# Attention into two mixtures of experts: which queue starts the small layout transfers, and which the stores of finished rows

## The chip, the cores and the metric

The kernel runs on one core of one Trainium2 chip. Times are microseconds (us) that the device took for the whole program. Five engines work side by side, each through its own instructions in order: TensorE (PE, with its weight loads as PEld), VectorE (DVE), ScalarE (ACT), GpSimd (POOL) and SyncE (SP). DMA transfers are started by an instruction on SP, ACT or POOL and then run on the core's 16 DMA engines; "to landing" is the time from that instruction to the arrival of the last byte. "Granted clock" is the share of its full speed that TensorE was given in a stretch.

## The reference, cut to what matters

A linear recurrence with complex decay runs over 768 tokens for 4 batches of 8 heads of 48 channels. Its output, as 3072 rows of 384, goes through a mixture of 8 experts and then a second one with a skip rule:

```python
for t in range(S):
    ar, ai = (a_re_n[:, :, t, :, None], a_im_n[:, :, t, :, None])
    new_re = ar * S_re - ai * S_im
    new_im = ar * S_im + ai * S_re
    kv = np.einsum('bhd,bhe->bhde', k[:, :, t], v[:, :, t])
    S_re, S_im = (new_re + kv, new_im)
    y[:, :, t] = np.einsum('bhd,bhde->bhe', q[:, :, t], S_re)
x = np.ascontiguousarray(y.transpose(0, 2, 1, 3)).reshape(B * S, H * D)
x = _moe_ref(x=x, **moe_kwargs)       # argmax expert, relu(x @ w1[e]) @ w2[e], times gate
return _moe2_ref(x=x, **moe2_kwargs)  # rows with x @ w_skip > 0 alone: x + the same
```

## The kernel before

**Stages.** `prefix` forms the running products P of the decays, up to about 165 us of the span. `attention` follows, up to about 389 us, where its last store starts. Then come the first and the second mixture of experts. The change lies in `attention`.

**Attention.** The tokens are cut into 12 units of 256 (the loop's n, three per batch), each of two chunks of 128 (24 steps i). For each unit `prod(n)` makes, on DVE and ACT, Qo = q·P and Ko = k/P, with channels on the partitions in an order in which three blocks of 128 hold eight heads. For the scores, TensorE needs the same numbers with 96 partitions (real and imaginary part of one head below each other) and the head as an index: the second layout, `qst` and `kst`. `relayout` makes it by transfers within the on-chip memory, five for each of the two parts: two of 48 partitions x 3 heads (144 KB), one of 32 partitions (64 KB) and two of 16 partitions (16 KB each). They are numbered 0 to 9; numbers 3, 4, 8 and 9 are the 16 KB ones. `qst` has three buffers, `kst` two.

**One step i** of the loop (line 692): state update on PE (`kv`), turning of Ko (`ktr`), the rows of the chunk before (`rows`, tile yp), the decay of the state on DVE (tiles Vt, T, St; it needs the chunk-end products `pb`), the scores of the next chunk (`scores`, tile sc, line 562, which needs all of that unit's `kst` and `qst`), their masks on DVE (sm), the store of the chunk before (`store`: xtp, xo, and a transfer to memory), and the turning of the state (`turn_state`: Stp, Ssb). Between these pieces the loop draws pieces of `prod(n + 2)`, called `fill`: unit n + 2 is made while unit n runs, Ko at the end of it.

**Queues.** SP starts all relayout transfers but five of unit 0 (`QP`, line 56). POOL starts the loads of k, q, v and pb and the stores of rows 0 to 19 (line 659); SP starts the last four stores. In the built program a transfer of SP or ACT takes the next of eight semaphores, one of POOL the next of another eight, and each waits until the earlier transfer on its semaphore has landed. Instructions of one queue start in order, so what waits for DVE or PE holds up what stands behind it.

Of the kernel before, what the change touches and what calls it, by code (L numbers as in the profile page):

```python
# [52 lines left out]
H0,H1=(6, 2)  # L53
HV=2
WU=4
QP,KP=({0: (5, 6, 7, 8, 9), 2: ()}, {2: ()})
FAST=((0, 2, 0, 7), (2, 3, 2, 4), (2, 4, 2, 2), (7, 4, 0, 0))
R_LATE, R_H1, R_H2, I_T, R_T, R_H3, H6, H9, H11, EF, EP = (3, 0.3, 1.5, 5, 2.5, 1.2, 5, 9, 11, 20, 3)
TAIL=2
# [4 lines left out]
XS=20  # L64
# [362 lines left out]
def attention(nc, tc, k, early, split):  # L427

    P = k.P
    with ExitStack() as c0:  # L430
# [208 lines left out]
        def store(i):  # L639

            x = X[i]
            for pair in range(4):
                nc.tensor.matmul(
                    lgb[32 * pair:32 * pair + E, 0:128], k.wgp[:, pair], x.xt[:, pair], start=True, stop=True,
                    tile_position=(0, 32 * pair))
            x.lt = wk.tile([128, 128], F32, name="lt", tag="lt", bufs=1)
            nc.scalar.activation(out=x.lt, in_=lgb[:, 0:128], func=AF.Copy)
            ps = psA.tile([128, 4, 2, 64], F32, name="xtp", tag="xt")
            for pair in range(4):
                nc.tensor.transpose(  # L650
                    ps[:, pair].rearrange("p r d -> p (r d)")[:, 0:112], x.xt[:, pair], k.idn[:112, :112])
            if i == XALT:
                xo = ip.tile([128, C, UG], F32, name="xo", tag="k").rearrange("p t g -> p (t g)")[:, 0:384]
            else:
                pool, tag = (wk, "xo") if i < ni - 1 else (up, "D0")
                xo = pool.tile([128, 384], F32, name="xo", tag=tag, bufs=1)
            nc.scalar.activation(  # L657
                out=xo.rearrange("p (a r d) -> p a r d", a=4, r=2), in_=ps[:, :, :, 0:48], func=AF.Copy)
            (nc.sync if i >= XS else nc.gpsimd).dma_start(out=k.x0[i * 128:i * 128 + 128], in_=xo)  # L659

        def logits(i):
            nc.tensor.matmul(lgb[:, 128:136], X[i].lt, k.sum4, start=True, stop=True)
# [29 lines left out]
        for i in range(ni):  # L692
# [37 lines left out]
            if i > 0:  # L730
                store(i - 1)
# [9 lines left out]
        emit(islice(split, SA[3]))  # L741
        logits(ni - 2)
        store(ni - 1)
        emit(islice(split, SA[4]))
        logits(ni - 1)
# [1193 lines left out]
```

## Time and profile before

| | us |
|---|---|
| median of 3 timed runs | 750.12 |
| the three runs | 747.13, 750.12, 752.61 |
| the profiled execution | 753.02 |
| its span, first to last instruction | 751.3 |
| PE busy | 638.0 (85%) |
| DVE busy | 600.3 (80%) |
| ACT busy | 425.3 (57%) |
| POOL busy | 203.7 (27%) |
| mean granted TensorE clock | 0.926 |

All rows below are from one profiled execution; times in them count from the start of its span. Busy time on an engine says how long it worked, not whether anyone waited for it; who waited is read from the chain of waits and from the idle time in square brackets behind an instruction, with what ended it. SP and POOL are listed with the instructions that start transfers.

### The profile page before, as it was taken

How to read it: one execution, taken by the hardware profiler on the slowest of the kernel's cores; microseconds unless marked ns; L12 is line 12 of the kernel's file. 1: busy time of each engine (PE TensorE's matmuls, PEld its weight loads, DVE VectorE, ACT ScalarE, POOL GpSimd, SP SyncE). 2: the span in 40 equal slices, each digit the busy share in tenths (PEclk: the TensorE clock that was granted, in tenths of full speed). 3: DMA queues.
4: the chain of work that ended last, by engine and by line, in shares of the span. 5: the costliest groups of instructions: out<-in, count | busy, mean ns of one | idle time of the engine just before them, and what ended most of it. 6: DMA issues, size and time to landing. Idle time of an engine off the chain costs nothing.

```text
span 751.3 us, 13960 instructions
## 1 busy us (share of the span) xinstructions
PE 638.0 (85%) x5007; PEld 550.5 (73%) x5007; DVE 600.3 (80%) x1391; ACT 425.3 (57%) x847; POOL 203.7 (27%) x296
## 2 busy tenths in 40 slices
PE   1787886515999979999978999999999999899991
PEld 0444444313888868887868899999999997678991
DVE  5989999995898967999878876566776668789980
ACT  7757786623356543554363365566655566488860
POOL 6200000004023221221534254334474443520110
PEclk9989998855699996999988999999999999999996
DMA  5769945008579886886634021263111148488900
GB/s 213 273 193 295 296 137 168 1 0 208 147 201 239 227 218 139 231 214 175 201 133 178 23 64 43 71 233 150 43 43 43 43 168 330 162 295 318 324 37 12
DMA packets 46045, 121.94 MB, mean 162 GB/s; under 512 B 12104, under 2 KB 30962, under 8 KB 41616
## 3 DMA queue, kind: packets, MB, share of 16 engines
q1 hardware_dynamic: 31200, 71.52, 31.3%
q0 software_dynamic: 14768, 49.45, 20.4%
q8 instruction: 41, 0.67, 0.4%
q14 instruction: 36, 0.29, 0.1%
HBM read 116.84 MB, written 16.52 MB: 178 GB/s over the span
## 4 chain that ended last, share of the span: by engine, by line
PE 53%; DVE 14%; DMA 11%; issue 9%; ACT 8%; POOL 2%; SPq 1%; POOLq 0%; DVEq 0%; ACTq 0%
PE yps L1402 13%; PE hps L1355 11%; PE sc L562 6%; DMA out_dram<-z,idx 5%; DVE t L381 3%; PE m L278 3%; PE yp L632 2%; PE yp L634 2%; DMA kst<-Ko 2%; PE wps L592 2%; DVE P L386 2%; PE wps L591 2%; PE xtp L650 1%; PE u L278 1%; PE ktp L546 1%
## 5 line engine op out<-in xcount | busy, mean ns | idle before, releaser
L149 DVE TENSOR_TENSOR wlo<-wraw,whi 128x768 fp32r<-128x768 f32 (+1 forms) x95 | 82.5, 903 | 13.8 <-ACT whi L148 12.8
L149 DVE TENSOR_TENSOR w<-P,w 128x768 fp32r<-128x768 f32 (+1 forms) x95 | 82.5, 903 | 11.0 <-ACT w L148 10.1
L278 PE MATMUL m<-sq,idn 128*128 128x288 f32 x112 | 40.0, 486 | 42.2 <-ACT sq L271 42.2
L148 ACT ACTIVATE whi<-wraw 128x768 fp32r<-128x768 f32 (+1 forms) x95 | 71.0, 802 | 0.0
L148 ACT ACTIVATE w<-P 128x768 fp32r<-128x768 f32 (+1 forms) x95 | 70.7, 800 | 0.0
L1362 DVE SCALAR_TENSOR_TENSOR hl<-hps,hh 128x512 fp32r<-128x512 f32 x48 | 33.1, 690 | 46.0 <-ACT hh L1361 45.9
L562 PE MATMUL sc<-qst,kst 96*128 96x128 f32 x384 | 56.4, 303 | 12.0 <-DMA kst<-Ko 9.7
L562 PEld LDWEIGHTS sc<-qst,kst 96*128 96x128 f32 x384 | 50.5, 210 | 18.1 <-issue 8.1
L1361 ACT ACTIVATE hh<-hps 128x512 fp32r<-128x512 f32 x48 | 28.7, 598 | 61.9 <-PE hps L1355 61.9
L278 PEld LDWEIGHTS m<-sq,idn 128*128 128x128 f32 x112 | 22.2, 216 | 55.1 <-ACT sq L271 29.6
L381 DVE TENSOR_TENSOR t<-P,n 128x288 f32<-128x288 f32 x127 | 57.7, 454 | 4.4 <-ACT n L332 1.9
L1390 POOL DMA_INDIRECT out_dram<-y,idx x26 | 28.0, 1076 | 111.5 <-ACT y L1389 95.4
L553 ACT ACTIVATE kt<-ktp 128x384 f32<-128x384 f32 x40 | 19.5, 488 | 59.5 <-PE ktp L552 59.4
L1402 PE MATMUL yps<-w,hh 128*128 128x394 f32 x192 | 51.4, 349 | 0.0
L1355 PE MATMUL hps<-xh,w 128*128 128x256 f32 x288 | 46.3, 295 | 4.0 <-DVE hl L1362 2.8
L1355 PEld LDWEIGHTS hps<-xh,w 128*128 128x128 f32 x288 | 41.0, 200 | 4.7 <-DVE hl L1362 3.0
L568 DVE TENSOR_TENSOR sm<-sc,tri 128x512 f32<-128x512 f32 x48 | 32.6, 680 | 12.6 <-PE sc L562 12.2
L467 POOL DMA_DIRECT2D qst<-Qo x5 | 2.8, 559 | 146.2 <-DVE D L503 146.2
L659 POOL DMA_DIRECT2D x<-xo x20 | 11.3, 565 | 108.3 <-ACT xo L657 108.3
L386 DVE TENSOR_TENSOR P<-t 128x144 f32<-128x144 f32 x127 | 37.9, 299 | 0.1
L496 DVE TENSOR_TENSOR Qo<-q,P 128x516 f32<-128x516 f32 (+5 forms) x52 | 36.7, 784 | 0.0
L632 PE MATMUL yp<-sm,v 128*64 128x128 f32 (+1 forms) x384 | 36.5, 279 | 0.0
(372 smaller groups left out, 1888.4 us busy)
## 6 DMA issues: line engine op xcount, KB each, us to landing
P<-in_w2t_dram SPq DMA_DIRECT2D x8, 1536.0 KB, 6.7
P<-in_v_dram SPq DMA_DIRECT2D x8, 1536.0 KB, 7.9
wraw<-in_v_dram SPq DMA_DIRECT2D x8, 1536.0 KB, 8.4
raw<-in_a_dram SPq DMA_DIRECT2D x15, 576.0 KB, 5.8
kst<-Ko SPq DMA_DIRECT2D x48, 144.0 KB, 3.7
qst<-Qo SPq DMA_DIRECT2D x46, 144.0 KB, 5.5
k<-in_k_dram POOLq DMA_DIRECT2D x12, 384.0 KB, 6.3
q<-in_q_dram POOLq DMA_DIRECT2D x12, 384.0 KB, 7.6
```

What stands on the lines that cost most here:

```text
L148: self.nc.scalar.activation(out=hi, in_=r, func=AF.Copy)
L149: self.nc.vector.tensor_tensor(lo, r, hi.bitcast(F32), op=ALU.subtract)
L278: nc.tensor.matmul(x, k.idn, sq[:, h, :, r], start=r == 0, stop=last and r == 1)
L381: nc.vector.tensor_tensor(t1, P.at(t - 1)[:, ::-1].unsqueeze(2).to_broadcast([128, 2, 2, G]), pairs, op=ALU.mult)
L386: nc.vector.tensor_tensor(P.at(t), t1[:, 0], t1[:, 1], op=ALU.add)
L496: nc.vector.tensor_tensor(V(Qo[:, r])[:, s], P4(d.q[:, s]), P4(p[:, :, r]), op=ALU.mult)
L562: nc.tensor.matmul(ps[:, h], U[n].kst[:, 4 * g + h, cs], U[n].qst[:, 4 * g + h, cs], start=True, stop=True)
L568: nc.vector.tensor_tensor(X[i].sm[:, 4 * g:4 * g + 4], X[i].sc[g], k.mask.to_broadcast([128, 4, 128]), op=ALU.mult)
L632: nc.tensor.matmul(o, U[n].v[:, c, h * 48:h * 48 + M], x.sm[:, h], start=zero, stop=True)
L1355: nc.tensor.matmul(ps[:, i], self.W.w1(s, wp_, j)[:, f * 128:f * 128 + 128], x[xp_][:, j], start=n == 0, stop=n == 8)
L1362: nc.vector.scalar_tensor_tensor(out=hl, in0=ps, scalar=0.0, in1=hh.bitcast(F32), op0=ALU.max, op1=ALU.subtract)
L1402: nc.tensor.matmul(ps, hs[kk // 2][hp][:, kk % 2, us], self.W.w2(s, wp_, kk, Weights.DW), start=n == 0, stop=n == 23)
```

## The change

The four 16 KB transfers of each relayout go from SP's queue to POOL's, for Q of units 1 to 11 and for K of all 12 units: 92 transfers. Unit 0's Q keeps its five on POOL. The 20 stores of rows that POOL started are now started by ACT. Nothing is computed otherwise.

```diff
-QP,KP=({0: (5, 6, 7, 8, 9), 2: ()}, {2: ()})
+SMALL = (3, 4, 8, 9)
+QP,KP=({0: (5, 6, 7, 8, 9), 2: SMALL}, {2: SMALL})
...
-            (nc.sync if i >= XS else nc.gpsimd).dma_start(out=k.x0[i * 128:i * 128 + 128], in_=xo)
+            (nc.sync if i >= XS else nc.scalar).dma_start(out=k.x0[i * 128:i * 128 + 128], in_=xo)
```

Line numbers behind line 56 grow by one. Three places show how the instructions now stand.

POOL at the start of attention, before (pd are the chunk-end products on their way to memory, pb their copies coming back; the first k and q are unit 2's, the second unit 3's):

```order
L467 DMA qst<-Qo 48x3x256 x2
L467 DMA qst<-Qo 32x512
L467 DMA qst<-Qo 16x256 x2
L406 DMA pd<-e_sb 48x1x384
L454 DMA pb<-pd 64x2x384
L454 DMA pb<-pd 48x2x384
L454 DMA pb<-pd 64x2x384
L454 DMA pb<-pd 48x2x384
L443 DMA k<-in_k_dram 128x768
L443 DMA q<-in_q_dram 128x768
L443 DMA k<-in_k_dram 128x768
L443 DMA q<-in_q_dram 128x768
```

And now, from pd on:

```order
L407 DMA pd<-e_sb 48x1x384
L468 DMA qst<-Qo 16x256 x4
L468 DMA kst<-Ko 16x256 x4
L455 DMA pb<-pd 64x2x384
L455 DMA pb<-pd 48x2x384
L455 DMA pb<-pd 64x2x384
L455 DMA pb<-pd 48x2x384
L444 DMA k<-in_k_dram 128x768
L444 DMA q<-in_q_dram 128x768
L468 DMA qst<-Qo 16x256 x4
L444 DMA k<-in_k_dram 128x768
L444 DMA q<-in_q_dram 128x768
```

Four transfers of kst of unit 0 now stand ahead of pd; pb and the k and q of unit 2 stand behind qst and kst of unit 1, and unit 3's k and q behind qst of unit 2.

POOL in one unit of the loop, before:

```order
L659 DMA x_61<-xo 128x384
L448 DMA v<-in_v_dram 128x768
L454 DMA pb<-pd 64x2x384
L454 DMA pb<-pd 48x2x384
L659 DMA x_61<-xo 128x384
L443 DMA k<-in_k_dram 128x768
L443 DMA q<-in_q_dram 128x768
```

And now:

```order
L468 DMA kst<-Ko 16x256 x4
L449 DMA v<-in_v_dram 128x768
L455 DMA pb<-pd 64x2x384
L455 DMA pb<-pd 48x2x384
L468 DMA qst<-Qo 16x256 x4
L444 DMA k<-in_k_dram 128x768
L444 DMA q<-in_q_dram 128x768
```

The two stores are gone; the loads of k and q wait behind qst (that is, for Qo) where they waited behind a store.

ACT at the end of a step, now (xo is the copy of the finished rows, Ssb that of the turned state, D the first step of a unit's `prod`):

```order
L648 ACTIVATE lt<-lgb 128x128
L658 ACTIVATE xo<-xtp 128x384
L660 DMA x_61<-xo 128x384
L618 ACTIVATE Ssb<-Stp 96x448
L489 ACTIVATE D_2205<-P_153 128x516
```

The store is the one new row; on PE and DVE no instruction moves. SP keeps six transfers of each relayout where it had ten.

## Rows read from the trace of the kernel before

**Rows 1.** Stretches: PE, PEld, DVE, ACT, POOL busy (count), clock, DMA share, GB/s.

```profile
200.00:217.80 17.80, 17.80 (x241) 15.57 (x240) 16.60 (x29) 9.21 (x21) 3.95 (x7) 1.00 0.69 174
...
262.70:278.60 15.90, 13.74 (x176) 11.97 (x176) 13.08 (x22) 8.47 (x19) 3.94 (x7) 1.00 0.83 209
278.60:295.70 17.10, 14.39 (x95) 12.27 (x96) 8.95 (x14) 4.56 (x11) 1.35 (x3) 0.50 0.60 145
```

**Rows 2.** Chain that ended last, 220 to 300: start, us, what.

```profile
225.34 1.98 PE sc L562 x16
...
231.35 1.98 PE sc L562 x16
...
238.47 1.98 PE sc L562 x16
...
274.69 7.34 DMA kst<-Ko
```

**Rows 3.** PE in order of time, scores alone: start, us, what, [idle before <-releaser].

```profile
270.47 2.05 PE L562 MATMUL sc<-qst,kst 96*128 96x128 f32 x16
...
279.31 0.77 PE L562 MATMUL sc<-qst,kst 96*128 96x128 f32 x2 [2.77 <-DMA kst<-Ko]
282.08 3.35 PE L562 MATMUL sc<-qst,kst 96*128 96x128 f32 x14 [2.01 <-DMA kst<-Ko]
...
294.51 2.60 PE L562 MATMUL sc<-qst,kst 96*128 96x128 f32 x16
```

**Rows 4.** SP in order of time, the relayouts of unit 6.

```profile
260.19 9.76 SPq L467 DMA_DIRECT2D qst<-Qo  x10
270.06 7.68 SPq L467 DMA_DIRECT2D kst<-Ko  x10
```

**Rows 5.** DVE in order of time, the second part of unit 6's Ko.

```profile
265.56 1.53 DVE L509 TENSOR_TENSOR Ko<-D,P 128x516 f32<-128x516 f32 x2
```

**Rows 6.** POOL in order of time, the loads between 270 and 276.

```profile
271.38 1.20 POOL L454 DMA_DIRECT2D pb<-pd  x2
...
274.79 0.55 POOL L443 DMA_DIRECT2D k<-in_k_dram  x1
```

**Rows 7.** Line 467 (relayout): duration in ns min/median/max, starts; landing.

```profile
L467 SPq DMA_DIRECT2D kst<-Ko x120: 507/620/1554, 173.4 to 360.6; - x120
...
L467 POOL DMA_DIRECT2D qst<-Qo x5: 496/519/657, 169.1 to 171.3; - x5
...
DMA to landing us min/median/max: 1.8/4.5/8.6
```

**Rows 8.** Waits of PE, 180 to 380: us in total, times, longest.

```profile
PE sc L562 <- DMA kst<-Ko: 9.7, 5, 4.3
```

**Rows 9.** POOL at the start of attention: q of unit 2.

```profile
178.66 0.55 POOL L443 DMA_DIRECT2D q<-in_q_dram  x1
```

**Rows 10.** DVE at the start of attention.

```profile
181.81 2.80 DVE L509 TENSOR_TENSOR Ko<-D,P 128x516 f32<-128x516 f32 x4
...
192.25 1.51 DVE L496 TENSOR_TENSOR Qo<-q,P 128x516 f32<-128x516 f32 x2
...
199.37 0.56 DVE L602 TENSOR_TENSOR Vt<-wps,pb 112x384 f32<-112x384 f32 x1 [1.32 <-PE wps L592]
...
201.44 0.35 DVE L607 TENSOR_TENSOR St<-T,Vt 112x192 f32<-112x192 f32 x1
```

**Rows 11.** PE at the start of attention.

```profile
181.98 0.77 PE L562 MATMUL sc<-qst,kst 96*128 96x128 f32 x2 [4.31 <-DMA kst<-Ko]
...
204.61 0.55 PE L615 MATMUL Stp<-idn,St 112*96 112x112 f32 x4
```

**Rows 12.** DMA issues: KB each, median us to landing.

```profile
q<-in_q_dram POOLq DMA_DIRECT2D x12, 384.0 KB, 7.6
```

**Rows 13.** Line 659 (stores), those that SP started.

```profile
L659 SPq DMA_DIRECT2D x<-xo x4: 332/342/352, 371.5 to 388.6; - x4
```

**Rows 14.** Waits of ACT, 180 to 380: us in total, times, longest.

```profile
ACT kt L553 <- PE ktp L552: 56.5, 27, 9.2
```

## The prediction, made before the changed kernel ran

> **What bounds the kernel now.** The change touches attention alone, so I read its stretches first, then the chain of waits through them, then the engines named there in order of time. Between 200.0 and 217.8 PE is busy for all of the 17.80 us at full clock, and DVE for 16.60 of them [rows 1]: PE sets the pace, DVE is close behind. In the chain, the scores of three successive steps start at 225.34, 231.35 and 238.47 [rows 2]; these are the steps at the end of a batch, which have less to do, and they take 6.01 and 7.12 us. The step that answers to them one batch later reads otherwise: scores at 270.47, the next ones at 279.31, and of these the last fourteen records only at 282.08, after idle times of 2.77 and 2.01 us that `kst` ended [rows 3]. The chain has there 7.34 us of a transfer into `kst` that SP started at 274.69 [rows 2]. From 278.6 to 295.7 the granted clock is 0.50, that is the lower of the two levels, 1.2 GHz [rows 1], after PE had stood. So one late `kst`, unit 6's, costs twice.
>
> Why was it late? DVE had the second part of Ko ready at 265.56 + 1.53 = 267.09 [rows 5]. SP was still busy with Q of the same unit, ten transfers from 260.19 on, and began with K at 270.06, ten more over 7.68 us [rows 4]. By then POOL started pb at 271.38 and k at 274.79 [rows 6], and K's last transfers ran beside those loads. SP's starts are the queue that unit 6 waited for.
>
> **The change, part by part.**
>
> *SP: 92 starts fewer.* A start takes 0.62 us at the median [rows 7], a relayout of ten 6.2 us, one of six 3.7. For unit 6: Q's six are through before K's data are there at 267.1; K's second part then needs three starts, the last at 267.1 + 2 x 0.62 = 268.3, or 272.8 landed at the median of 4.5, and 276.9 at the longest of 8.6 [rows 7]. The scores need it at 270.47 + 6.01 = 276.5 [rows 2, 3]. It is in time at the median by 3.7 us, and 0.4 late at the worst. What this is worth:
> - The wait: the step's scores ended at 282.08 + 3.35 = 285.43; without it at 276.5 + 2.05 = 278.5 [rows 3]. That is 6.9 us.
> - The clock: from the end of these scores to the next ones passed 294.51 - 285.43 = 9.1 us [rows 3]; one batch earlier, at full clock, 238.47 - (231.35 + 1.98) = 5.1 [rows 2]. That is 4.0 us more, if PE doesn't stand there any longer.
> - Other waits for `kst` inside the loop: of 9.7 us in all [rows 8], 4.8 are unit 6's [rows 3] and 4.3 are unit 0's [rows 11]; 0.6 is left.
>
> Together 11.5 us less. The bounds: from 2.5 us (four starts of 0.62 saved, and K still in the crowd of loads) to 11.5.
>
> *POOL: 92 starts more, 20 fewer.* At 0.52 us [rows 7] that is 48 us more over 200 us on an engine that was busy 3.95 of 17.8 [rows 1]: nothing in the loop, where the small transfers of K come before the unit's v and pb. k and q of unit n + 3 now wait for Qo of unit n + 2 instead of a store; both came in the same microseconds, and they are needed a unit later. Cost 0.
>
> *POOL at the start.* Here order matters. q of unit 2 was started at 178.66 [rows 9]. Now it stands behind unit 1's K, which DVE finishes at 181.81 + 2.80 = 184.61 [rows 10]: two small starts (1.0), four of pb (2.4, at 0.60 each [rows 6]) and k (0.55) later q starts at 188.6, ten microseconds later than before, and lands at the median of 7.6 us [rows 12] at 196.2. DVE wanted it at 192.25 [rows 10]: 4.0 us late, with everything behind it on DVE. Of these DVE makes up the 1.32 us that it stood before Vt at 199.37, so St, done at 201.44 + 0.35 = 201.8, comes at 204.5 [rows 10]. PE turns that state at 204.61 [rows 11]. So it is just hidden, and DVE works off the rest at about 1.2 us in two steps (17.80 - 16.60 [rows 1]). In exchange the first scores lose most of their 4.31 us wait [rows 11], because pb, k and q no longer run beside unit 0's K; that lead ends at the same St. I take 0 for the start. Bounds: 3 us gained, if St doesn't hold PE; 8 us lost, if the 4.0 pass on to PE in full and the standing costs another stretch of low clock at unit 6's price of 4.0.
>
> *ACT: 20 starts more.* SP's stores took 0.34 us each [rows 13], so 6.8 us in all, in front of Ssb and of the next unit's squares. ACT waits 2.1 us on average (56.5 / 27) before each kt that it waits for [rows 14]; the start fits in there. Cost 0; with the longest relayout start, 1.55 us [rows 7], it would still fit. The store's semaphore was last used a relayout earlier, and the next xo is a step away, so no new wait is on its path.
>
> **The sum.** 753.0 - 11.5 = 741.5 us against the profiled execution, which lies 2.9 above the median of the runs shown and 0.4 above the highest. Against the median it gives 738.6. I predict **740**.
>
> **Rivals.**
> *The 16 DMA engines set the landing, not SP.* From 262.7 to 278.6 their share is 0.83 [rows 1], the last K transfer needed 7.34 us [rows 2] against a median of 4.5, and the bytes stay. Then only the starts are saved: 2.5 us at unit 6, the low clock stays, time 750. Against it: K would start and mostly land before pb and k do [rows 5, 6]. The Trainium skill says this in DMA: Bandwidth & Descriptors, section "Issuing engines are not separate DMA queues": transfers of all issuing engines share the 16 engines, and issuing from several saves only the issue time, usually small beside the transfer. Here the trace agrees only in part: ten starts at 0.62 us are longer than the median landing of 4.5. By the page alone the result would be "no change". Chance 0.16.
> *The start costs.* POOL's new order makes DVE 4 us late and PE feels it: 741.5 + 4 to 8 = 745.5 to 749.5. For it: DVE has only 1.2 us in 17.8 to spare. Against: the state is turned late enough. Chance 0.14.
> *ACT becomes the bound: slower.* In-order ACT holds kt, xt and Ssb behind a store's start. If that took longer than the 2.1 us of slack, each microsecond more would cost 20; 1% slower than the median (757.6) is reached at a hold of 2.1 + (757.6 - 741.5) / 20 = 2.9 us, and at 3.5 us it is 769.5. For it: no ACT start is in the trace at all. Against it: SP's take 0.34, and no start of a relayout of K over 1.55 [rows 7, 13]. Chance 0.08.
> *K's wait moves to another unit*, with a new place and the same 11 us: 753. Chance 0.04.
> The forecast keeps 0.58.
>
> **How the numbers follow.** 1% of 750.1 is 7.5 us, about what a measurement of this kernel can tell from no change: faster means below 742.6, slower above 757.6. The forecast, with its offset to the median, is 736 to 743 and nearly all faster; both middle rivals and the moved wait are within 1%, the ACT rival is slower, to which I add 0.02 for what I haven't seen. Faster 0.57, same 0.33, slower 0.10. The range goes down to 734 (the start's 3 us gained, and a little more), and up to 752, which takes in the first two rivals and leaves out the slow one.
>
> **What will show it.** SP's relayouts take about 4 us each, with gaps between them; unit 6's K starts within 1 us of Ko; the scores of the step after 270 stand under 1 us; no stretch at 0.50 begins between 270 and 300; the wait of PE for `kst` falls from 9.7 to under 3 us. At the start, DVE's first Qo of unit 2 is released by q of unit 2, some 3 to 5 us later than before, and the state turned at 204.61 moves by under 1 us. ACT's store start is under 0.7 us. I am wrong if unit 6's K starts early and yet lands after its scores want it, if the late q moves PE by several microseconds, or if a low clock shows up in another place.

## The result, and the profile after

The changed kernel takes **743.65 us** (median of 12 runs, 742.09 to 747.09) against 751.58 for the kernel before in the same job (12 runs, 745.38 to 755.61): ratio 0.9909 [0.988, 0.9939]. That is 7.9 us less at the medians, where 11.5 were summed. The ratios, with their 95% intervals, are estimated apart from the medians and leave out executions over 1.5% above the fastest of their kernel, so they are not quite the quotients of the medians. The profiled execution took 745.46 us; its span is 743.7 us, against 751.3 before, and its mean granted clock 0.932 against 0.926.

At unit 6 the profile shows what was forecast, though the queue held K back in a way that the prediction did not name. The stretches of [rows 1], the same columns, in the changed kernel:

```profile
200.00:217.80 17.80, 17.80 (x240) 15.57 (x241) 17.34 (x29) 9.45 (x22) 8.14 (x16) 1.00 0.85 218
262.70:278.60 15.90, 15.90 (x204) 13.99 (x203) 14.71 (x25) 8.39 (x20) 6.83 (x13) 1.00 0.87 232
278.60:295.70 17.10, 16.89 (x221) 14.57 (x219) 16.08 (x27) 9.53 (x23) 7.17 (x14) 1.00 0.96 238
```

PE no longer stands in the second stretch, and the third has the clock at 1.00 (2.4 GHz) instead of 0.50. Note the first: DVE is now busy for 17.34 of 17.80 us, where it was 16.60.

SP in order of time at unit 6, which answers to [rows 4]:

```profile
256.94 4.29 SPq L468 DMA_DIRECT2D qst<-Qo  x6
265.05 4.29 SPq L468 DMA_DIRECT2D kst<-Ko  x6
```

Q's six starts end 3.8 us before K's begin; K no longer queues behind Q, and its second three starts wait only for DVE, which has that part of Ko at 265.42 + 1.54 = 266.96 (267.09 in [rows 5]). The scores on PE, which answer to [rows 3]:

```profile
269.74 2.05 PE L563 MATMUL sc<-qst,kst 96*128 96x128 f32 x16
...
275.74 2.05 PE L563 MATMUL sc<-qst,kst 96*128 96x128 f32 x16
...
282.86 2.05 PE L563 MATMUL sc<-qst,kst 96*128 96x128 f32 x16
```

The step after 269.74 comes 6.00 us later and in one piece. Its end is 277.79 instead of 285.43, and the next scores start at 282.86 instead of 294.51: **11.65 us gained** by there. PE's waits from 180 to 380 (us, times, longest), beside [rows 8]:

```profile
PE Stp L616 <- DVE St L608: 5.1, 1, 5.1
...
PE lgb L905 <- DVE aoh L899: 1.2, 1, 1.2
...
PE sc L563 <- DMA kst<-Ko: 0.2, 1, 0.2
```

The wait for `kst` has gone from 9.7 to 0.2 us. Two larger ones are new in attention: 5.1 us for St at the start, and 1.2 us for `aoh`, a tile of the routing.

**What had held SP.** SP's own waits in the kernel before, 180 to 380 (us, times, longest):

```profile
SPq L467 <- DMA qst<-Qo: 8.6, 8, 2.7
...
SPq L467 <- DMA kst<-Ko: 6.7, 9, 2.0
```

The longest of them lies at unit 6. By the trace's semaphore records, the ninth of Q's ten starts, at 268.77, waited on semaphore 101, which Q's first, started at 260.19, signals when it has landed; that was at 268.75. SP stood for 2.67 us before that start. K began 2.97 us after the second part of its data was there (270.06 - 267.09), so the greater part of that was this wait and not time spent on starting: with ten starts and eight semaphores, the ninth takes the first one's. In the changed kernel, with six starts, SP's waits in the same stretch have one for a relayout transfer, of 0.3 us.

**Where gain was given back: the routing.** After step 16 of the scores PE needs `aoh` for the first batch's routing. PE in the kernel before:

```profile
318.84 2.05 PE L562 MATMUL sc<-qst,kst 96*128 96x128 f32 x16
...
321.58 0.33 PE L904 MATMUL lgb<-aoh,onesb 128*128 128x96 bf16 x1
...
327.66 0.60 PE L562 MATMUL sc<-qst,kst 96*128 96x128 f32 x3
```

and in the changed kernel:

```profile
307.29 2.05 PE L563 MATMUL sc<-qst,kst 96*128 96x128 f32 x16
...
311.07 0.33 PE L905 MATMUL lgb<-aoh,onesb 128*128 128x96 bf16 x1 [1.19 <-DVE aoh L899]
...
318.67 1.49 PE L563 MATMUL sc<-qst,kst 96*128 96x128 f32 x11
```

From the scores to the next took 8.82 us; now it takes 11.38, or 2.6 more. DVE's last operation on `aoh`, in the kernel before:

```profile
321.26 0.26 DVE L898 TENSOR_TENSOR aoh<-aoh,rs_fm 128x96 bf16<-128x96 bf16 x1
```

and in the changed kernel:

```profile
310.75 0.26 DVE L899 TENSOR_TENSOR aoh<-aoh,rs_fm 128x96 bf16<-128x96 bf16 x1
```

It started 2.42 us after the scores' start, and now 3.46. DVE's order of work is the same. In the kernel before PE had stood for unit 6's K, and DVE was 1.04 us further ahead. Behind the new wait comes a stretch near the lower clock level, with the columns of [rows 1]:

```profile
312.10:315.60 3.50, 3.45 (x32) 2.72 (x33) 2.46 (x8) 1.72 (x4) 1.09 (x3) 0.51 0.77 185
```

**And in the expert part.** The chain that ended last, at four places that answer to each other, before:

```profile
596.07 8.63 PE yps L1402 x48
...
639.72 4.38 PE yps L1251 x24
...
736.59 0.97 POOL out_dram L1470
```

and after:

```profile
586.28 8.63 PE yps L1403 x48
...
609.38 12.06 DMA out_dram<-y,idx
...
636.91 4.39 PE yps L1252 x24
...
735.01 0.93 POOL out_dram L1471
```

The lead is 9.79 us at the first place, 2.81 at the second and 1.58 at the last scatter; from there the program ends 14.7 us later before (751.3 - 736.59) and 8.7 after, with no work in either trace that explains the difference (in the other traces it is 7.1 to 13.0 us). Most of the 7 us between the first two places stands at a scatter that landed after 12.06 us. GpSimd's next scatter waited for that, and PE for the `ro` behind it on GpSimd. PE's wait for it between 590 and 660, 0.8 us before:

```profile
PE acc L1002 <- POOL ro L1020: 5.9, 2, 5.5
```

So the profiled pair's 7.6 us are 11.65 gained, about 2 lost up to 586 (the routing's 2.6 and small shifts), 8.2 lost between 586 and 735, and 6.0 got back in the drain at the end.

### The profile page after: what moved, and what is told of

It reads as the page before. It is cut to its first block, busy times and chain, and to the rows that moved or that the text cites. A ratio compares the mean times of both kernels' runs of the same rounds, so it can differ in the third digit from the quotient of the medians.

```text
span 743.7 us, 14051 instructions
## 1 busy us (share of the span) xinstructions
PE 634.7 (85%) x5007; PEld 548.1 (74%) x5007; DVE 599.5 (81%) x1391; ACT 425.5 (57%) x847; POOL 240.3 (32%) x368
## 4 chain that ended last, share of the span: by engine, by line
PE 46%; DVE 19%; DMA 12%; ACT 9%; issue 9%; POOL 3%; SPq 0%; POOLq 0%; DVEq 0%; ACTq 0%
PE yps L1403 12%; PE hps L1356 11%; DMA out_dram<-z,idx 6%; PE sc L563 4%; DVE t L382 4%; PE m L279 3%; DMA out_dram<-y,idx 2%; DVE P L387 2%; PE yp L633 2%; DVE Qo L497 2%; PE yp L635 2%; PE wps L592 1%; DVE Ko L510 1%; PE wps L593 1%; PE xtp L651 1%
## 5 line engine op out<-in xcount | busy, mean ns | idle before, releaser
L150 DVE TENSOR_TENSOR w<-P,w 128x768 fp32r<-128x768 f32 (+1 forms) x95 | 82.6, 904 | 11.5 <-ACT w L149 10.6
L468 POOL DMA_DIRECT2D qst<-Qo x49 | 24.5, 505 | 179.2 <-DVE D L504 149.8
L563 PE MATMUL sc<-qst,kst 96*128 96x128 f32 x384 | 53.1, 294 | 2.1 <-DMA kst<-Ko 1.2
L563 PEld LDWEIGHTS sc<-qst,kst 96*128 96x128 f32 x384 | 48.1, 203 | 7.2 <-issue 4.7
L468 POOL DMA_DIRECT2D kst<-Ko x48 | 23.5, 495 | 52.7 <-DVE sm L569 27.3
L510 DVE TENSOR_TENSOR Ko<-D,P 128x516 f32<-128x516 f32 (+5 forms) x52 | 36.0, 784 | 0.1
L279 PE MATMUL u<-sq,idn 128*128 128x288 f32 x112 | 35.6, 445 | 0.0
```

The source lines that it names most:

```text
L150: self.nc.vector.tensor_tensor(lo, r, hi.bitcast(F32), op=ALU.subtract)
L279: nc.tensor.matmul(x, k.idn, sq[:, h, :, r], start=r == 0, stop=last and r == 1)
L468: (nc.gpsimd if 5 * r + i in pool else nc.sync).dma_start(out=to, in_=x)
L510: nc.vector.tensor_tensor(V(Ko[:, r])[:, s], P4(D2[0][:, s]), P4(p[:, :, r]), op=ALU.mult)
L563: nc.tensor.matmul(ps[:, h], U[n].kst[:, 4 * g + h, cs], U[n].qst[:, 4 * g + h, cs], start=True, stop=True)
```

## The experiments

Times are medians with the lowest and highest; ratios are to runs of the kernel before on the same chip in the same job.

| run | us | ratio |
|---|---|---|
| small transfers only | 740.48 (736.82 to 743.29) | 0.9899 [0.9845, 0.9952] |
| stores only | 784.32 (779.35 to 794.44) | 1.0546 [1.0457, 1.0635] |
| changed + SP starts dummies | 781.05 (777.58 to 787.79) | 1.0442 [1.0395, 1.0488] |
| changed, first units' small ones on SP | 737.06 (735.11 to 737.93) | 0.9862 [0.9822, 0.9903] |
| small only + SP starts dummies | 748.51 (742.87 to 754.41) | 0.9966 [0.9912, 1.002] |
| small only, first units' on SP | 740.12 (736.57 to 749.02) | 0.9824 [0.9728, 0.9921] |
| changed, again | 742.01 (739.19 to 753.07) | 0.9894 [0.9859, 0.993] |
| changed, hook at step 15 | 747.94 (745.54 to 751.0) | 0.9971 [0.9937, 1.0005] |
| changed, `aoh` early | 738.09 (737.58 to 742.59) | 0.9822 [0.9757, 0.9887] |
| small only, first units' on SP, `aoh` early | 737.2 (736.15 to 741.34) | 0.9802 [0.9735, 0.9868] |
| K's small ones only | 736.63 (731.76 to 738.35) | 0.9774 [0.9703, 0.9846] |
| changed, a third time | 743.74 (741.21 to 746.39) | 0.9889 [0.9828, 0.995] |

### The two halves of the change

The small transfers alone; the early stores stay on GpSimd:

```diff
-            (nc.sync if i >= XS else nc.scalar).dma_start(out=k.x0[...], in_=xo)
+            (nc.sync if i >= XS else nc.gpsimd).dma_start(out=k.x0[...], in_=xo)
```

> The 92 small transfers on GpSimd, the 20 stores left there as before. Queue theory (SP's starts made unit 6's K late): nearly all of the change is in the small transfers; 7 to 9 us under before, PE's wait for kst in the loop under 2 us, no stretch at half clock from 278 to 296. Store theory (the stores' place matters): 4 us or less under before, because GpSimd now carries 112 starts and the loads of k and q wait behind stores as well.

740.48 us. The whole gain is in the small transfers; of the two numbers that of the queue came out. The scores of unit 6 read as in the changed kernel (269.84, 275.84, 282.96), and PE has no wait for `kst` among its listed ones.

The stores alone:

```diff
-QP,KP=({0: (5, 6, 7, 8, 9), 2: SMALL}, {2: SMALL})
+QP,KP=({0: (5, 6, 7, 8, 9), 2: ()}, {2: ()})
```

> The 20 stores on ScalarE, all small transfers left on SP. Queue theory: unit 6's K starts at 270 and lands at 284 as before, the half-clock stretch stays; within 3 us of before. Store theory: 4 us or more under before. If a store's start held up ScalarE, it would be slower than before by 3 us or more.

784.32 us, 35.7 more than the kernel before in that job (748.67): a miss for both theories. Slower by 3 us or more was written for a hold on ScalarE; the hold that the trace shows is on SP. SP's longest wait from 180 to 380 (us, times, longest):

```profile
SPq L467 <- DMA x<-xo: 48.9, 10, 8.8
```

One relayout of K on SP, in order of time:

```profile
221.44 15.19 SPq L467 DMA_DIRECT2D kst<-Ko  x10
```

SP's relayout starts wait 48.9 us for the landing of stores that ScalarE started, and PE then 19.5 us for `kst`. Nothing in the data joins these transfers. What joins them is the semaphore that each signals at its end: SP's and ScalarE's transfers take theirs from one set in turn, so a start on SP has to wait for an older store that had the same one. The trace's semaphore records show it for two of these waits: K's start at 236.12 waited on semaphore 105, the one of the store started at 229.47, which landed at 236.10; the one at 258.63 waited on 102, for the store of 251.99 that landed at 258.61. Ten starts then occupy SP for 15.19 us, where unit 6's slow ones took 7.68 before [rows 4].

### Is it SP's starts, or what the DMA engines move?

The changed kernel, in which SP starts a 64-byte transfer into a tile that nothing reads (`pad`, a column of it each) in place of each one that left it:

```diff
                     (nc.gpsimd if 5 * r + i in pool else nc.sync).dma_start(out=to, in_=x)
+                    if pool is SMALL and 5 * r + i in pool:
+                        c = next(pads)
+                        nc.sync.dma_start(out=pad[0:16, c:c + 1], in_=x[:, 0:1])
```

> The changed kernel, with a transfer of 64 bytes (16 values of Qo or Ko into a tile that nobody reads) started by SP in the place of each small one that moved away: SP's starts are those of before, the bytes on its queue are not. Queue theory: unit 6's K starts 3 us late again, lands after 280, and the time goes back to before, within 3 us. Engines theory (the load on the 16 DMA engines sets the landing): the 64 bytes cost nothing, the time stays with the changed kernel, 6 us or more under before.

781.05 us, neither number. SP's waits from 180 to 380 have the stores again:

```profile
SPq L471 <- DMA x<-xo: 22.0, 6, 6.0
SPq L468 <- DMA x<-xo: 19.3, 4, 12.4
```

With ten starts in a relayout and the stores on ScalarE, this coupling covers what was asked. So once more with the stores on GpSimd:

> The small transfers on GpSimd's queue, the early stores on GpSimd's queue as in the kernel before, and SP starts a 64-byte transfer into an unread tile in place of each small transfer that left it. Queue theory (SP's ten starts in a row are what counts): back to the kernel before, 750 us, ratio 1.00 +- 0.006, unit 6's K late again by some 6 us. Engines theory (what the 16 DMA engines move sets the landing): the useful transfers are placed as in the first experiment, so 740 to 742 us, ratio 0.99. If the 35 us of the two slow experiments came from starts on SP alone and not from the stores on ScalarE, 780 us here too.

748.51 us, ratio 0.9966: back at the kernel before within the uncertainty, as the queue theory has it, while the useful transfers are issued as in the run at 740.48 (0.9899 [0.9845, 0.9952]; the two intervals overlap a little, and the trace decides). And 32.5 us less than with the stores on ScalarE (there 1.0442, in another job): the coupling belongs to the pair (ten starts on SP, stores on ScalarE), not to the starts alone. The loss has moved, though, and unit 6's K, which the queue theory named, is in time. SP in order of time at unit 4, with the dummies in between:

```profile
237.31 2.54 SPq L468 DMA_DIRECT2D kst<-Ko  x3
239.89 2.66 SPq L471 DMA_DIRECT2D pad<-Ko  x2
242.65 2.08 SPq L468 DMA_DIRECT2D kst<-Ko  x3
```

the scores that wanted that K, on PE:

```profile
248.01 3.64 PE L568 MATMUL sc<-qst,kst 96*128 96x128 f32 x16 [0.91 <-DMA kst<-Ko]
...
262.70 1.49 PE L568 MATMUL sc<-qst,kst 96*128 96x128 f32 x11
```

and the stretch behind them, with the columns of [rows 1]:

```profile
248.00:262.50 14.50, 14.39 (x110) 12.60 (x110) 9.70 (x18) 4.09 (x10) 2.75 (x6) 0.53 0.69 180
```

K is late by 0.91 us, and the two scores are 14.7 us apart, where the changed kernel needs 8.2 (245.77 to 253.99): 6.5 us for 0.91 us of waiting, with the clock at its lower level from 248.89 to 262.55. This is the same double price as unit 6 paid, without the wait being large. It doesn't follow every such wait: in the same execution PE stood 1.07 us for `kst` at 317.50 and 1.20 for `aoh` at 321.08, and the granted clock was 1.00 from 262.55 to 385.43.

The dummies also bring back the waits of the ninth start. SP's, 180 to 380:

```profile
SPq L471 <- DMA qst<-Qo: 6.0, 6, 2.1
...
SPq L471 <- DMA kst<-Ko: 3.8, 4, 1.2
```

One of them, 1.56 us at 242.05, stands ahead of the second half of the late K. So the run shows that ten starts cost the gain, and not how much of it is the time to start and how much the wait for a landing; the latter depends on what the DMA engines carry.

Which half of the starts? Only K's small transfers on GpSimd, the stores too:

```diff
-QP,KP=({0: (5, 6, 7, 8, 9), 2: SMALL}, {2: SMALL})
+QP,KP=({0: (5, 6, 7, 8, 9), 2: ()}, {2: SMALL})
```

> Only K's small transfers on GpSimd's queue; Q's small ones from unit 2 on stay on SP, the early stores stay on GpSimd's queue. SP then starts ten of Q and six of K. The prediction has K as the late one, with SP held by the ten starts of Q and the ten of K behind them: if K's own starts carry it, most of the gain stays (741 to 744 us, ratio 0.989 to 0.993, no wait for kst over 1 us); if Q's starts ahead of K carry it, K of some unit is still late by 1 us or more and the clock falls once: 747 to 750 us.

736.63 us, below both of the expected ranges: K's own starts carry it, and Q's ten ahead of them don't hurt. PE has no wait for `kst` among its listed ones. SP at unit 6:

```profile
255.59 6.93 SPq L468 DMA_DIRECT2D qst<-Qo  x10
263.66 4.36 SPq L468 DMA_DIRECT2D kst<-Ko  x6
```

Q no longer stands behind K of unit 5, whose starts end at 254.05, and is through before K's begin. Its ten take 6.93 us here, where they took 9.76 [rows 4]; SP's waits for Q's landings are 4.0 us in all, the longest 1.3. This is the lowest median of the versions run, not apart from the two with `aoh` early: below the changed kernel of the same job (743.74) by 7.1 us, and no run of the two overlaps. Its trace still has the loss at the routing (1.58 us of waiting for `aoh`); K alone with `aoh` early was not run.

### The start

Unit 0's K and unit 1's small transfers left on SP, first with the stores on ScalarE, then on GpSimd:

```diff
-QP,KP=({0: (5, 6, 7, 8, 9), 2: SMALL}, {2: SMALL})
+QP,KP=({0: (5, 6, 7, 8, 9), 1: (), 2: SMALL}, {0: (), 1: (), 2: SMALL})
```

> The changed kernel, but unit 0's K and unit 1's Q and K keep their small transfers on SP, so that pb and unit 2's q and k start as early as before. If the late q and pb at the start are hidden, as I summed: within 1.5 us of the changed kernel, state turned at 204 to 205. If they cost: 3 to 5 us under the changed kernel. If the lead of the first scores was worth something: 1 to 3 us over it.

> The small transfers of units 2 to 7 on GpSimd's queue, those of unit 0's K and unit 1's Q and K left on SP, the early stores on GpSimd's queue. If the 16 small starts ahead of unit 2's q load cost something at the start, as the run with stores on ScalarE hints: 737 us or less, ratio 0.985 or less; if they are hidden, as the prediction has it: as the first experiment, 740 to 741 us, ratio 0.99.

737.06 and 740.12 us. The first has no run of the changed kernel in its job; its ratio, 0.9862 [0.9822, 0.9903], overlaps with the changed kernel's in another (0.9909 [0.988, 0.9939]). The second stands beside the changed kernel of its own job:

> The changed kernel once more, on the same chip and against the same runs of the kernel before, to set the versions with the first units on SP and with a later hook against it: 741 to 744 us, ratio 0.991.

742.01 us, ratio 0.9894 [0.9859, 0.993], against 0.9824 [0.9728, 0.9921]: the intervals overlap, and so do the runs. In the second one's trace the first scores wait 5.02 us for `kst` again, and the scores of step 2 start at 203.50, against 201.20 in the changed kernel. Whether the start is worth anything stays open.

### The time given back at the routing

The first batch's routing, which is mixed into attention from step 14 on, one step later:

```diff
-EARLY_HOOK = (14, 19)
+EARLY_HOOK = (15, 19)
```

> The changed kernel with the first batch's routing starting at step 15 instead of step 14 (EARLY_HOOK 15). If the 2.6 us given back between scores steps 15 and 17 come from the routing meeting a VectorE that no longer runs ahead: step 16 to 17 takes about 9 us instead of 11.4, the end of attention comes 2 us earlier, 741 us against 743.5 for the changed kernel in the same job. If the 2.6 us only follow the routing to wherever it stands: the same loss one step later, and no difference over 0.5 us.

747.94 us, slower than the changed kernel of that job. PE in order of time:

```profile
312.91 2.05 PE L563 MATMUL sc<-qst,kst 96*128 96x128 f32 x16
...
316.45 0.33 PE L905 MATMUL lgb<-aoh,onesb 128*128 128x96 bf16 x1 [1.49 <-DVE aoh L899]
...
324.83 3.78 PE L563 MATMUL sc<-qst,kst 96*128 96x128 f32 x16
...
337.55 2.05 PE L563 MATMUL sc<-qst,kst 96*128 96x128 f32 x16
```

Steps 16 to 17 are clean (305.38 to 312.91, 7.53 us), and the wait for `aoh` stands one step on, with 11.9 and 12.7 us for two steps that take 6.0 and 7.1 without it. The loss goes where the routing goes, and costs more among the short steps; this placement was a bad one, and it doesn't tell the cause. The next run does: DVE makes `aoh` ahead of other work that it did first.

```diff
-        yield
-        ex = self.scratch(sh, "ex")
-        nc.scalar.activation(out=ex, in_=w, func=AF.Exp)
         fm = self.scratch([128, T, 1], "fm")
         v.tensor_reduce(out=fm, in_=oh, axis=AX.X, op=ALU.max)
         v.tensor_tensor(oh, oh, fm.to_broadcast(sh), op=ALU.is_equal)
+        yield
+        ex = self.scratch(sh, "ex")
+        nc.scalar.activation(out=ex, in_=w, func=AF.Exp)
```

> The changed kernel with two VectorE operations of the routing (rs_fm and the second aoh, 0.5 us together) placed ahead of the two St and the first half of Ko instead of behind them; nothing else moves in attention. Give-back theory (what the freed time was lost to between scores steps 16 and 17 is TensorE's wait for aoh on a VectorE that no longer runs ahead, and the half-speed stretch behind it): no wait for aoh there, no half-speed stretch, step 16 to 17 in 9 us or less instead of 11.4, attention's end 2.5 to 4 us earlier, 739 to 741 us and 2.5 us less than the changed kernel in the same job. Rival (the loss belongs to the routing's place, whatever VectorE does): step 16 to 17 stays over 11 us, same time as the changed kernel.

738.09 us, 5.6 less than the changed kernel of the job. PE:

```profile
305.77 2.05 PE L563 MATMUL sc<-qst,kst 96*128 96x128 f32 x16
...
308.31 0.33 PE L905 MATMUL lgb<-aoh,onesb 128*128 128x96 bf16 x1
...
314.38 0.82 PE L563 MATMUL sc<-qst,kst 96*128 96x128 f32 x5
```

No wait, and 8.61 us from scores to scores instead of 11.38: the wait was for DVE's place in the order. The intervals of the two ratios touch (0.9822 [0.9757, 0.9887] and 0.9889 [0.9828, 0.995]), so the trace is the firmer evidence for the 2.8 us. The comparison run, the changed kernel a third time, gave another look at the same thing:

> The changed kernel in the same job, to set the three others against it: 741 to 744 us, ratio 0.99.

743.74 us. In this execution unit 7's K was late:

```profile
290.06 3.33 PE L563 MATMUL sc<-qst,kst 96*128 96x128 f32 x14 [1.17 <-DMA kst<-Ko]
...
313.57 0.33 PE L905 MATMUL lgb<-aoh,onesb 128*128 128x96 bf16 x1 [0.15 <-DVE aoh L899]
```

PE stood for 1.17 us, the scores (288.40 to 302.60) are 14.2 apart, and after that the routing's step takes 8.83 us (310.82 to 319.65), with 0.15 of waiting for `aoh`. So here, as in the kernel before, a K late between 260 and 300 us goes with a routing that is nearly free. In the eight traces with no such late K and `aoh` in its old place (the two with long SP waits for stores left aside), PE waits 1.2 to 1.9 us for `aoh`. The changed kernel's third job also shows what is late next: unit 7's K, though SP had only six starts for it.

All together: small transfers from unit 2 on, stores on GpSimd, `aoh` early:

> Small transfers of units 2 to 7 on GpSimd's queue, those of unit 0's K and unit 1's on SP, the early stores on GpSimd's queue, and the two routing operations ahead as in the run before it. If the gains add: 735 to 738 us, ratio 0.982 +- 0.004, faster than the changed kernel of the same job by 4 us or more. If the first units' place was noise: as the run before it, 739 to 741 us.

737.2 us. That is the number written for gains that add, but the run with `aoh` early alone came out at 738.09, below the 739 written for it, and the two don't separate: whether the first units' place adds anything isn't shown.

## Why the prediction was right, and where it was not

**SP's starts and unit 6: right in place and in size, incomplete in what held SP.** 11.65 us at the scores of 282.86 against 11.5 summed. The wait and the small waits before it come to 285.43 - 277.79 = 7.64 (6.9 + 0.6 summed), the clock to 4.0 (4.0 summed). K began with the first part of Ko, and the wait for `kst` fell to 0.2, all as listed. A start took 0.60 us on SP (0.62 before), by the durations of line 468. The prediction took the 9.76 us of Q's ten starts for time spent on starting; at its own 0.62 us they make 6.2, and 2.67 of the rest were the wait for the landing of the first. The run with K alone refines it further: it is K's own starts that had to leave.

**The DMA engines as the limit: not borne out as a rival.** With the bytes of the changed kernel and SP's starts given back, the gain was gone (748.51 against 740.48). The Trainium skill (DMA: Bandwidth & Descriptors, section "Issuing engines are not separate DMA queues") puts the saving of several issuing engines at the issue time, usually small beside the transfer. The trace agrees in part. Four starts of 0.60 us fewer in a relayout are such a saving, and not a small one here, since 11.65 us hung on K's being in time; but 2.67 of the 2.97 us by which unit 6's K began late were the wait for a landing. That landing, 8.56 us after its start, is where the engines' load comes in; no run varied the load by itself.

**The start: 0, right in size, partly by luck.** DVE, which answers to [rows 10]:

```profile
192.68 0.56 DVE L603 TENSOR_TENSOR Vt<-wps,pb 112x384 f32<-112x384 f32 x1 [6.90 <-DMA pb<-pd]
...
195.51 1.51 DVE L497 TENSOR_TENSOR Qo<-q,P 128x516 f32<-128x516 f32 x2 [0.40 <-DMA q<-in_q_dram]
```

and PE, beside [rows 11]:

```profile
195.16 0.98 PE L616 MATMUL Stp<-idn,St 112*96 112x112 f32 x4 [5.14 <-DVE St L608]
...
204.50 0.55 PE L616 MATMUL Stp<-idn,St 112*96 112x112 f32 x4
```

Qo of unit 2 starts 3.26 us later (4.0 summed), and the state turned at 204.61 is turned at 204.50. But q itself held DVE for 0.40 us alone. What the prediction did not see is that pb, ahead of q on GpSimd, holds DVE first, for 6.90 us, and PE for 5.14; the lead from the earlier first scores paid for it, and that the two came out even was not worked out beforehand.

**ACT: 0 here, but the rival had the wrong mechanism.** A store's start took 0.34 us, by the durations of line 660. "No new wait is on its path" looked at ScalarE, and even there two waits are listed as ended by a store, before the squares of a next unit, of 4.3 us together; that they cost nothing is inferred from the run with the stores left on GpSimd, which is no faster by its ratio. The larger wait that the stores make stands on SP, and only the six starts that are left there keep it out of the changed kernel's profile; with ten it cost 32.5 and 35.7 us.

**The sum: the step that failed.** "753.0 - 11.5" carried the gain at unit 6 unreduced to the end of the program, and named no cover that PE's standing gave to others. It gave one: DVE's lead at the routing, worth 2.6 us. In the expert part a second loss of 7 us stands, in the profiled pair partly repaid by a shorter drain. One of the signs it had given for being wrong came up: a low clock in another place, from 312.14 to 315.55. Forecast 740, measured 743.65: inside the range and in the forecast direction, but above the 742.6 that it had set as the bound for faster. In the profiled pair luck is in it as well: without the 6.0 us of the drain, which nothing here explains, 1.6 would be left of the gain.

**Open:** the scatter. GpSimd's second gather of rows ahead of it, in the changed kernel:

```profile
600.11 1.02 POOL L1325 DMA_INDIRECT xg<-x,idx  x1 [1.79 <-PE hps L1356]
```

It is held 1.79 us, where the one of the kernel before, at 608.41, is held 0.30, and the weights' gathers start later and stand before the scatter. This is so in each of the six traces in which GpSimd has the 92 small transfers and ScalarE the stores (the changed kernel three times, with the hook moved, with `aoh` early, with the dummies; PE's longest wait for `ro` is 4.5 to 6.4 us), and in none of the other eight (0.4 to 2.3). The order of instructions is the same there, and so are the semaphores: in both kernels of the pair the two gathers signal 108 and 109. In the changed kernel GpSimd issues nothing from 598.32 to 599.89, and a transfer of 8 KB of instructions runs from 599.45 to 599.89; in four of the other five traces such a transfer ends within 0.12 us of the end of the pause, and in the one with the dummies none is recorded. That suggests a wait for code, whose place would shift with the number of instructions ahead; no run tried it, and the cause stays open. That K alone is 7 us faster than the changed kernel fits with its absence.

## What to carry to other kernels

Count starts per queue and per deadline, not bytes alone, and count them against the semaphores that they take in turn: with ten starts and eight semaphores, the ninth start of a relayout waited for the landing of the first. It sufficed to move the small ones of the tile that is last ready. When a stall goes, list the engines that ran ahead during it, since their lead goes too. And move a transfer to another queue only after reading who shares a completion semaphore with it.

## What the runs showed that was not expected

- In this program, stores started by ScalarE hold SP's starts: 48.9 us of SP waits in ten pieces, up to 8.8 us, and 784.32 us of time; with six starts a relayout on SP no such wait is listed in the changed kernel and one of 3.1 us in the run with the hook at step 15; with dummies to make it ten they are back (22.0 and 19.3 us).
- A wait of 0.91 us of PE was followed by 14.5 us at a clock of 0.53 and cost 6.5 us; one of 1.19 by 3.5 us at 0.51. Waits of 1.07 and 1.20 us in another place were followed by no lower clock.
- In the kernel before, SP's relayout starts waited 15.3 us for the landing of SP's own earlier relayout transfers, 2.67 of it in front of unit 6's K; with six starts a relayout 0.3 us is left in the profiled run of the changed kernel, and at most 2.8 in its other two.
